# Keys in blocks of 128 and shared remainders in a three-stage attention kernel on one Trainium2 core

## The chip, the cores and the metric

The kernel runs on one core of a Trainium2 chip. The metric is the device time of one execution in microseconds (us); the median of the runs is compared. The engines are called by the names of the profile: PE multiplies matrices, DVE and POOL do elementwise work, ACT evaluates functions such as tanh and exp, SP issues most DMAs. DVE, ACT and POOL each work through their queue in order.

## What is computed

Three layers follow one another, all in float32. The first is soft-capped attention over 4 batches and 12 heads, 448 positions, 64 features per head. The second mixes four single-head causal attentions ("experts") of the 768 features, of which two are kept per position. The third is a gated feed-forward layer with a product along the positions.

```python
scores = scale * np.matmul(q, k.transpose(0, 1, 3, 2))      # (4, 12, 448, 448)
scores = cap * np.tanh(scores / cap)
attn = np.exp(scores - np.max(scores, axis=-1, keepdims=True))
attn = attn / (np.sum(attn, axis=-1, keepdims=True) + 1e-09)
x = np.matmul(attn, v)            # heads side by side: (4, 448, 768)
q, k, v = x @ wq[e], x @ wk[e], x @ wv[e]                   # per expert e
out += mask[..., None] * w * (softmax(causal(q @ k.T / 8)) @ v @ wo[e])
h = gelu(x @ w_in); u, v = halves of h                      # third layer
gated = u * (einsum('ts,bsd->btd', w_sg, layernorm(v)) + b_sg)
return x + gated @ w_out
```

## The kernel before

The unit of the first layer is a pair of heads: 24 pairs, six to a batch. The features of the two heads lie in the lower and the upper 64 partitions of one tile (`qp`, `kp`), so that two products of 64 rows each, one per head, can stand in the array at once. Scores are computed transposed, keys by queries. The 448 keys are cut into four blocks of 112 (`CP`, `NC`).

`slot(i, side)` (line 253) is one step of the program, and its calls write the order of the queues out by hand; until the end of the first layer PE, DVE, ACT and POOL keep the order in which the calls stand (`InOrder`, `pin`). Slot i holds: the first two key blocks of pair i (`scores(..., 0, ...)`, line 192), with a tanh per block and one exp for both; the values of pair i - 1 (`values`, line 219), in which four blocks of 112 keys are accumulated for both heads into one tile `po`; the last two blocks of pair i; after each second pair a product with a one-hot matrix (`sums`, line 230) that adds up the exp over the keys; and the additions of the four blocks of exp into `pb` (`add_up`, line 214). The first of them, block 0 plus block 1, stands in `scores` (line 208): it is done by DVE in batch 0 and by POOL after it. The other two are done by DVE.

Between these stand the calls `side("a")`, `side("w")`, `side("p")` and `side("n")`, which put the rest of the program into the slots. In slots 0 to 9 (`prepare_weights`, line 574) that is the product of `wo` and `w_in`: DVE turns twelve units of 64-bit words into float32 (`convert`, six kinds of operation, tiles `wi..m`, `wi..e`), and PE multiplies them (`products`, tiles `w2ps`), by the tables `turns`, `u_loads` and `u_products`. From slot 10 on it is the second layer of the batch before (`PLAN`, line 481): `queries_keys` (tiles `qk`), `values_chunk` (`v`), `weigh` (`a`, `pe`), `turn` (`tr`, `pt`), `attend` (`av`).

`normed` (line 318) takes a finished batch from the first layer to the second. `invert` takes the reciprocal of the sums, writes it to DRAM and reads it back spread over partitions (`rb`); `over_sums` multiplies the attention output `os` by it; `in_parts` splits the result into a rounded part `xh` and a rest `xl`, three pieces of two feature blocks each. The products `qk` read `xh` and `xl` and begin in slot 10 (for batch 0).

After the last slot (24) the order is no longer held by hand: `experts_end` (line 559) and the third layer (`mlp_a`, `mlp_b`, `mlp_c`) are interleaved, and a scheduler sets the order. PSUM, the memory that PE writes to, is divided into two two-bank tiles for scores (`ps_s`), one bank for `po` (`ps_o`) and three for all else (`ps_g`, tag "g").

The lines that fix the shape of the work:

```python
mm(s[:CP, j, :S], kp[r, c * CP:(c + 1) * CP], qp[r, :], start=True, stop=True)      # scores
mm(po[64 * j:64 * j + 64, :S], vv[:, j, c, :], pend[b, hp][c // 2][:, j, c % 2, :], # values
   start=(c == 0), stop=(c == NC - 1))
(dve if b == 0 else pool_e).tensor_tensor(pb, p[:, :, 0, :], p[:, :, 1, :], op=ALU.add)
```

Of the kernel before, what the change touches and what calls it, by code (L numbers as in the profile page):

```python
# [22 lines left out]
HP = H // 2  # L23
# [5 lines left out]
CP, NC = 112, 4  # L29
EPS = 1e-9  # L30
# [42 lines left out]
def build(ctx: ExitStack, tc: tile.TileContext, a: dict):  # L73
# [55 lines left out]
    onehot = const.tile([CP, 3, 32], F32, name="onehot")  # L129
# [47 lines left out]
    os_t, sums_t, pend, rb_d = {}, {}, {}, {}  # L177

    def load_pair(b, hp):

        qp = at.tile([128, S], F32, tag="qp", name=f"qp{b}_{hp}", bufs=3)
        kp = at.tile([128, S], F32, tag="kp", name=f"kp{b}_{hp}", bufs=3)
        vv = at.tile([CP, 2, NC, D], F32, tag="vv", name=f"vv{b}_{hp}", bufs=3)
        nc.sync.dma_start(kp, a["kT"][b, :, hp, :])
        nc.sync.dma_start(qp, a["qT"][b, :, hp, :])
        if (b, hp) == pairs[0]:
            scale()
            load_w(0)
        nc.sync.dma_start(vv, a["v"][b, :, 2 * hp:2 * hp + 2])
        return qp, kp, vv  # L190

    def scores(b, hp, h, qp, kp):

        p = at.tile([CP, 2, 2, S], F32, tag="p", name=f"p{b}_{hp}_{h}", bufs=4)
        for c2 in range(2):
            c = 2 * h + c2
            s = ps_s.tile([128, 2, 512], F32, tag="s", name=f"s{b}_{hp}_{c}")
# [16 lines left out]
    def add_up(b, hp):
        _, p, pb = pend[b, hp]
        for c2 in range(2):
            dve.tensor_tensor(pb, pb, p[:, :, c2, :], op=ALU.add)

    def values(b, hp, vv):
        po = ps_o.tile([128, 512], F32, tag="po", name=f"po{b}_{hp}")  # L220
# [690 lines left out]
```

## Time and profile before

| | us |
|---|---|
| median of 3 runs | 558.57 |
| lowest, highest | 557.87, 561.39 |
| the profiled execution | 559.72 |
| span of its trace | 558.0 |

The span runs from the first to the last instruction of the program; the profiled execution's own time lies 1.7 us above it. A row of a view names the engine, the operation and the tiles as out<-in. Line 119 of the kernel is the helper that issues every matmul, line 104 the one for all of DVE, ACT and POOL, so groups are told apart by their tiles. A float32 matmul shows as two instructions. Ends of matmuls are modelled and overlap, so the distance from start to start is what a group costs PE.

### The profile page before, as it was taken

To read this page: it belongs to the slowest core of one execution; us is meant where nothing else is said; L and a number is where in the kernel's file an instruction comes from. 1 tells how busy PE (TensorE), PEld (TensorE's weight loads), DVE (VectorE), ACT (ScalarE), POOL (GpSimd) and SP (SyncE) were. 2 spreads that over 40 slices of the span, in tenths; PEclk is the share of its full clock that TensorE was granted. 3 is DMA by queue.
4 is the path that set the end of the run, shared out by engine and by line. 5 is a ranking of instruction groups with operands and counts; after the bars stand their busy time and mean duration, and the time that the engine had idled before them with its cause. 6 is when DMAs were issued, how large, how long until landed. Compare 5 with 4: busy or idle time off the path is not lost.

```text
span 558.0 us, 7562 instructions
## 1 busy us (share of the span) xinstructions
PE 532.7 (95%) x2732; PEld 346.3 (62%) x2732; DVE 361.4 (65%) x725; ACT 325.7 (58%) x508; POOL 141.4 (25%) x180
## 2 busy tenths in 40 slices
PE   7999999899999989999988989999999989999997
PEld 2333333455555554656557655878768879889996
DVE  3899999984666636567567599676631786485300
ACT  5988888688687896577822345353534344253211
POOL 0000122141155251243340364515521131031000
PEclk9999999999999999999999978999999999999999
DMA  8974615752424141322056221010421000000111
GB/s 246 338 217 123 207 51 160 223 175 80 130 67 142 50 140 49 103 71 67 22 158 165 54 59 58 29 58 0 162 101 64 2 0 34 33 34 33 51 49 66
DMA packets 30596, 53.97 MB, mean 97 GB/s; under 512 B 3872, under 2 KB 22880, under 8 KB 30560
## 3 DMA queue, kind: packets, MB, share of 16 engines
q1 hardware_dynamic: 29408, 48.26, 28.2%
q0 software_dynamic: 1152, 5.24, 2.8%
q8 instruction: 21, 0.34, 0.3%
q14 instruction: 15, 0.12, 0.1%
HBM read 41.83 MB, written 11.67 MB: 96 GB/s over the span
## 4 chain that ended last, share of the span: by engine, by line
PE 73%; DVE 16%; ACT 6%; DMA 2%; issue 2%; POOL 1%; DVEq 0%; POOLq 0%; ACTq 0%; SPq 0%
PE o L119 15%; PE po L119 10%; PE s L119 10%; PE qk L119 8%; PE sp L119 7%; PE v L119 5%; ACT p L104 4%; PE a L119 3%; PE hv L119 3%; PE hu L119 3%; PE w2ps L119 2%; PE tr L461 2%; PE av L119 2%; DVE pb L104 2%; DVE rs L104 2%
## 5 line engine op out<-in xcount | busy, mean ns | idle before, releaser
L104 ACT ACTIVATE p<-s,tsc 112x896 f32<-112x896 f32 x96 | 91.4, 1005 | 24.4 <-PE s L119 24.4
L119 PE MATMUL s<-qp,kp 64*112 64x448 f32 x384 | 84.4, 557 | 3.4 <-ACT p L104 3.4
L104 ACT ACTIVATE p<-p,capt 112x1792 f32<-112x1792 f32 x48 | 85.9, 1790 | 1.3
L104 POOL TENSOR_TENSOR pb<-p 112x896 f32<-112x896 f32 x18 | 38.9, 2163 | 166.6 <-ACT p L104 96.9
L119 PE MATMUL po<-p,vv 112*64 112x448 f32 x384 | 77.3, 545 | 0.0
L104 DVE TENSOR_TENSOR pb<-pb,p 112x896 f32<-112x896 f32 x48 | 57.3, 1194 | 16.0 <-ACT p L104 12.3
L119 PEld LDWEIGHTS s<-qp,kp 64*112 64x112 f32 x384 | 30.8, 172 | 50.6 <-issue 21.3
L119 PEld LDWEIGHTS po<-p,vv 112*64 112x64 f32 x384 | 25.5, 136 | 45.0 <-issue 44.0
L104 ACT ACTIVATE pe<-a,m 112x112 f32<-112x112 f32 (+3 forms) x64 | 31.2, 491 | 25.3 <-DVE m L104 24.5
L104 POOL TENSOR_SCALAR pe<-pe,cs 112x112 f32<-112x112 f32 (+1 forms) x64 | 31.6, 519 | 50.3 <-DVE cs L104 50.2
L104 DVE CUSTOM_DVE_ANT_0 a<-a,neg 112x112 f32<-112x112 f32 (+3 forms) x64 | 27.7, 464 | 20.0 <-PE a L119 20.0
L119 PE MATMUL qk<-xh,wqk_h 128*128 128x448 f32 x96 | 38.2, 398 | 2.6 <-DVE xh L104 2.6
L119 PE MATMUL o<-gh,wu_h 128*128 128x448 f32 x96 | 35.6, 371 | 0.8 <-DMA wu_h<-wud 0.8
L119 PE MATMUL o<-gl,wu_h 128*128 128x448 f32 x96 | 35.6, 371 | 0.0
L119 PE MATMUL qk<-xh,wqk_l 128*128 128x448 f32 x96 | 35.4, 369 | 0.0
L119 PE MATMUL a<-qk 64*112 64x112 f32 (+3 forms) x128 | 29.9, 440 | 5.6 <-ACT pe L104 3.4
L119 PE MATMUL o<-gh,wu_l 128*128 128x448 f32 x96 | 35.0, 370 | 0.0
L104 ACT ACTIVATE ob<-o 128x448 f32<-128x448 f32 x24 | 13.0, 541 | 31.5 <-PE o L119 31.3
L119 PE MATMUL v<-wvg_h,xh 128*112 128x260 f32 x96 | 28.7, 299 | 0.7 <-ACT pe L104 0.7
L461 PE MATMUL tr<-ident,pe 112*112 112x112 f32 x160 | 23.7, 261 | 4.9 <-DVE lg L104 1.8
L119 PE MATMUL v<-wvg_h,xl 128*112 128x260 f32 x96 | 27.1, 283 | 0.0
L119 PE MATMUL v<-wvg_l,xh 128*112 128x260 f32 x96 | 27.1, 282 | 0.0
(226 smaller groups left out, 1096.5 us busy)
## 6 DMA issues: line engine op xcount, KB each, us to landing
kp<-in_kT_dram SPq DMA_DIRECT2D x24, 224.0 KB, 3.1
qp<-in_qT_dram SPq DMA_DIRECT2D x24, 224.0 KB, 3.2
vv<-in_v_dram SPq DMA_DIRECT2D x24, 224.0 KB, 3.1
rb<-rd SPq DMA_DIRECT2D x24, 224.0 KB, 4.7
out_dram<-ob SPq DMA_DIRECT2D x24, 224.0 KB, 1.9
wuw<-in_w_out_dram SPq DMA_DIRECT2D x8, 384.0 KB, 3.5
wud<-wuw SPq DMA_DIRECT2D x16, 192.0 KB, 1.9
ws<-in_wqk_dram SPq DMA_DIRECT2D x4, 384.0 KB, 6.0
```

What stands on the lines that cost most here:

```text
L104: ins = f(*args, **kw)
L119: pin(nc.tensor.matmul(*args, **kw))
L461: pin(nc.tensor.transpose(g[:CP, j * CP:(j + 1) * CP], pe[:, j * CP:(j + 1) * CP], ident))
```

## The change

The keys are cut into three blocks of 128 (`KT` is 384) and a remainder of 64. The remainders of an even pair and of the odd pair after it make one block, computed in the slot of the odd pair: even pair in the lower, odd pair in the upper 64 partitions of the scores. Its products have 64 rows and 64 columns, so four of them, two pairs by two heads, stand in quarters of the array. The values of a pair are computed two slots after its scores; those of an odd pair begin with the four quarter products, of which two finish `po` of the even pair and two open `po` of the odd pair. `po` of odd pairs lies in `ps_g`. A slot is added (slot 25) for the values of pair 23.

All additions into `pb` are done by DVE now: two for an even pair, four for an odd one, of which two have 64 partitions. In `normed`, batch 0 is taken over earlier, and in `prepare_weights` the products stand up to one slot earlier and `wt` is loaded ahead of the first units. The loads are put into other places of the slots; the values' remainder is a load of its own (`vl`).

```diff
+KT = S - S % 128
...
+    def load_v(i):
...
+        b, hp = pairs[i]
+        vv = at.tile([128, 2, KT // 128, D], F32, tag="vv", name=f"vv{i}", bufs=3)
         nc.sync.dma_start(vv, a["v"][b, :, 2 * hp:2 * hp + 2])
...
+        vl = None
+        if hp % 2:
+            vl = at.tile([128, 2, D], F32, tag="vl", name=f"vl{i}", bufs=2)
+            nc.sync.dma_start(vl, a["vl"][b, hp // 2])
...
+    def scores(i, h):
+        last = h == 1 and i % 2 == 1
+        n = 2 if h == 0 or last else 1
+        p = at.tile([128, 2, n, S], F32, tag=("p0", "p1" if n == 1 else "p2")[h], name=f"p{i}_{h}", bufs=(3, 1)[h])
+        pend[i] = (*pend.get(i, ()), p)
+        for c2 in range(n):
+            s = ps_s.tile([128, 2, 512], F32, tag="s", name=f"s{i}_{2 * h + c2}")
             for j in range(2):
                 r = slice(64 * j, 64 * j + 64)
+                if c2 and last:
+                    for half in range(2):
+                        qp, kp = qk_t[i - 1 + half]
+                        mm(s[64 * half:64 * half + 64, j, :S], kp[r, KT:], qp[r, :], start=True, stop=True)
+                else:
+                    qp, kp = qk_t[i]
+                    c = 2 * h + c2
+                    mm(s[:, j, :S], kp[r, c * 128:(c + 1) * 128], qp[r, :], start=True, stop=True)
+            act.activation(p[:, :, c2, :], s[:, :, :S], AF.Tanh, scale=tsc)
             yield 805.0
+        act.activation(p, p, AF.Exp, scale=capt)
...
+    def add_up(i, h):
+        p = pend[i][h]
         if h == 0:
+            pb = pbs[i] = at.tile([128, 2, S], F32, tag="pb", name=f"pb{i}", bufs=3)
+            dve.tensor_tensor(pb, p[:, :, 0, :], p[:, :, 1, :], op=ALU.add)
+            return
+        dve.tensor_tensor(pbs[i], pbs[i], p[:, :, 0, :], op=ALU.add)
+        if i % 2:
+            for half in range(2):
+                r, pb = slice(64 * half, 64 * half + 64), pbs[i - 1 + half]
+                dve.tensor_tensor(pb[r], pb[r], p[r, :, 1, :], op=ALU.add)
+    def values(i):
+        vv, vl = v_t.pop(i)
+        odd = i % 2
+        po = po_t[i] = (ps_g if odd else ps_o).tile([128, 512], F32, tag="g" if odd else "po", name=f"po{i}")
+        if odd:
+            b, hp = pairs[i]
+            p = pend[i][1]
+            for half in range(2):
+                r = slice(64 * half, 64 * half + 64)
+                for j in range(2):
+                    mm(po_t[i - 1 + half][64 * j:64 * j + 64, :S], vl[r, j, :], p[r, j, 1, :],
+                       start=(half == 1), stop=(half == 0))
+            os_t[b, hp // 2] = ao.tile([128, 2, S], F32, tag="os", name=f"os{i}", bufs=4)
+            act.activation(os_t[b, hp // 2][:, 0, :], po_t.pop(i - 1)[:, :S], AF.Copy)
+        for c in range(KT // 128):
             for j in range(2):
+                mm(po[64 * j:64 * j + 64, :S], vv[:, j, c, :], pend[i][c // 2][:, j, c % 2, :],
+                   start=(c == 0 and not odd), stop=(c == KT // 128 - 1 and odd == 1))
             yield 805.0
+        if odd:
+            act.activation(os_t[b, hp // 2][:, 1, :], po_t.pop(i)[:, :S], AF.Copy)
...
+        if i > 1:
+            drain(values(i - 2))
+        if here:
+            load_v(i)
         side("a")
...
+        if here:
+            add_up(i, 0)
+            drain(scores(i, 1))
...
-        elif step == (3, "w"):
+        elif step == ((3, "w") if b else (2, "a1")):
             over_sums(b, 0)
             over_sums(b, 1)
             load_rb(b, 2)
-        elif b == 0 and step == (3, "a1"):
+        elif b == 0 and step == (3, "w"):
             in_parts(b, 0)
             in_parts(b, 1)
-        elif step == (4, "w"):
-            if b:
-                in_parts(b, 0)
+        elif b == 0 and step == (3, "n"):
             over_sums(b, 2)
-            if not b:
-                in_parts(b, 2)
+            in_parts(b, 2)
+        elif b and step == (4, "w"):
+            in_parts(b, 0)
+            over_sums(b, 2)
         elif b and step == (4, "a1"):
             in_parts(b, 1)
...
-        u_products = [(), (), (0,), (1, 2), (3,), (4, 5), (6,), (7, 8), (9,), (10, 11)]
+        u_products = [(), (0,), (1,), (2,), (3, 4), (5,), (6, 7), (8,), (9,), (10, 11)]
```

How the instructions stand on an engine is shown at three places. The first is PE in slot 5 (pair 5 of batch 0). `s` are scores with the pair and the block in the name, `po` values; before, the name has the batch and the pair in it.

```order
L119 MATMUL s0_5_0_429<-qp5_297,kp5_298 112x448 x2
L119 MATMUL s0_5_1_433<-qp5_297,kp5_298 112x448 x2
L119 MATMUL po0_4_453<-p0_4_0_369,vv0_4_337 64x448 x4
L119 MATMUL po0_4_453<-p0_4_1_404,vv0_4_337 64x448 x4
L119 MATMUL s0_5_2_476<-qp5_297,kp5_298 112x448 x2
L119 MATMUL s0_5_3_480<-qp5_297,kp5_298 112x448 x2
```

The same slot in the changed kernel:

```order
L120 MATMUL s5_0_406<-qp5_342,kp5_343 128x448 x2
L120 MATMUL s5_1_410<-qp5_342,kp5_343 128x448 x2
L120 MATMUL po2_377<-p3_1_330,vl3_317 64x448 x2
L120 MATMUL po3_428<-p3_1_330,vl3_317 64x448 x2
L120 MATMUL po3_428<-p3_0_278,vv3_315 64x448 x4
L120 MATMUL po3_428<-p3_1_330,vv3_315 64x448 x2
L120 MATMUL s5_2_458<-qp5_342,kp5_343 128x448 x2
L120 MATMUL s5_3_462<-qp4_224,kp4_225 64x448
L120 MATMUL s5_3_462<-qp5_342,kp5_343 64x448
L120 MATMUL s5_3_462<-qp4_224,kp4_225 64x448
L120 MATMUL s5_3_462<-qp5_342,kp5_343 64x448
```

The odd slot has 10 score products and 10 value products, against 8 and 8 before; an even one has 6 and 6, so two pairs keep 16 and 16. Quarter products are the two rows that read `vl3` and the four of `s5_3`.

The second place is DVE in slots 7 and 8, from the first addition for pair 7 (before: pair 1 of batch 1) to the first product with `rb` of batch 0. Before:

```order
L104 TENSOR_TENSOR pb1_1_587<-pb1_1_587,p1_1_1_622 112x896 x2
L104 TENSOR_SCALAR wi11m_652<-wi1_5w_528 128x512
L104 TENSOR_SCALAR wi11m_652<-wi11m_652 128x512 x2
L104 SCALAR_TENSOR_TENSOR wi11m_652<-wi1_5w_528,wi11m_652 128x512
L104 TENSOR_SCALAR wi11e_653<-wi11m_652 128x512
L104 SCALAR_TENSOR_TENSOR wi11e_653<-wi1_5w_528,wi11e_653 128x512
L104 TENSOR_TENSOR wi11m_652<-wi11m_652,wi11e_653 128x512
L104 TENSOR_TENSOR wqk_l_76<-ws7_589,wqk_h_75 128x6x128
L104 COPY rs1_696<-sum1_0_691 128x448
L104 TENSOR_TENSOR pb1_2_662<-pb1_2_662,p1_2_1_679 112x896 x2
L104 TENSOR_TENSOR wqk_l_76<-ws8_664,wqk_h_75 128x6x128
L104 TENSOR_TENSOR os0_0_217<-os0_0_217,rb0_0_616 128x896
```

In the changed kernel:

```order
L105 TENSOR_TENSOR pb7_602<-p7_0_545 128x896
L105 TENSOR_TENSOR pb7_602<-pb7_602,p7_1_604 128x896
L105 TENSOR_TENSOR pb6_524<-pb6_524,p7_1_604 64x896
L105 TENSOR_TENSOR pb7_602<-pb7_602,p7_1_604 64x896
L105 TENSOR_SCALAR wi11m_639<-wi1_5w_513 128x512
L105 TENSOR_SCALAR wi11m_639<-wi11m_639 128x512 x2
L105 SCALAR_TENSOR_TENSOR wi11m_639<-wi1_5w_513,wi11m_639 128x512
L105 TENSOR_SCALAR wi11e_640<-wi11m_639 128x512
L105 SCALAR_TENSOR_TENSOR wi11e_640<-wi1_5w_513,wi11e_640 128x512
L105 TENSOR_TENSOR wi11m_639<-wi11m_639,wi11e_640 128x512
L105 TENSOR_TENSOR wqk_l_76<-ws7_564,wqk_h_75 128x6x128
L105 TENSOR_TENSOR os1_306<-os1_306,rb0_0_596 128x896
```

An odd pair has four additions where it had two, and the row that reads only `p7_0` was POOL's. The first product with `rb` moves ahead of pair 8's additions and of the second `wqk_l` row.

The third place is PE at the end of the first layer, from the last `sums` on. `a` are expert scores of batch 2, `hv` and `hu` the first products of the third layer. Before:

```order
L119 MATMUL sum3_2_2432<-pb3_5_2251,onehot_71 32x448 x2
L119 MATMUL a2_0_0_2_2491<-qk2_0_2197 112x336
L119 MATMUL a2_0_1_2_2492<-qk2_0_2197 112x336
L119 MATMUL a2_0_0_3_2516<-qk2_0_2197 112x448
L119 MATMUL a2_0_1_3_2517<-qk2_0_2197 112x448
L119 MATMUL hv0_0_2509<-w2_h_2462,yh0_2503 112x512
```

In the changed kernel:

```order
L120 MATMUL sum3_2_2418<-pb23_2271,onehot_71 32x448 x2
L120 MATMUL a2_0_0_2_2424<-qk2_0_2177 112x336
L120 MATMUL a2_0_1_2_2425<-qk2_0_2177 112x336
L120 MATMUL po22_2336<-p23_1_2273,vl23_2257 64x448 x2
L120 MATMUL po23_2436<-p23_1_2273,vl23_2257 64x448 x2
L120 MATMUL po23_2436<-p23_0_2208,vv23_2255 64x448 x4
L120 MATMUL po23_2436<-p23_1_2273,vv23_2255 64x448 x2
L120 MATMUL a2_0_0_3_2450<-qk2_0_2177 112x448
L120 MATMUL a2_0_1_3_2451<-qk2_0_2177 112x448
L120 MATMUL v2_2_2471<-wvg_h_77,xh2_2139 112x260
```

The values of pair 23 stand between the two steps of `weigh`; they were done one slot earlier.

## Rows read from the trace of the kernel before

**Rows 1.** The page, part 1: busy time, share of the span, instructions.

```profile
PE 532.7 (95%) x2732; PEld 346.3 (62%) x2732; DVE 361.4 (65%) x725; ACT 325.7 (58%) x508; POOL 141.4 (25%) x180
```

**Rows 2.** Busy time per stretch; columns: PE, PEld, DVE, ACT, POOL, clock, DMA, GB/s.

```profile
24.20:110.30 86.10, 83.51 (x359) 30.84 (x358) 83.03 (x113) 73.16 (x68) 10.97 (x5) 1.00 0.56 170
111.50:290.40 178.90, 174.65 (x1031) 99.35 (x1030) 108.76 (x246) 131.84 (x192) 60.65 (x62) 1.00 0.31 95
322.00:558.00 236.00, 225.09 (x1111) 187.69 (x1109) 134.76 (x293) 93.61 (x210) 60.00 (x93) 0.96 0.14 49
```

**Rows 3.** The chain that ended last, 60 to 125 us: start, length, what.

```profile
69.61 1.01 DVE pb L104
...
108.59 0.64 DVE xh L104
...
109.27 2.31 PE qk L119 x10
```

**Rows 4.** The timeline of PE, 60 to 73 us: start, length, instructions.

```profile
63.41 1.76 PE L119 MATMUL s<-qp,kp 64*112 64x448 f32 x8
65.10 1.98 PE L119 MATMUL w2ps<-wi6m,wt 128*128 128x512 f32 x4
67.02 0.96 PE L119 MATMUL sum<-pb,onehot 112*32 112x448 f32 x8
67.91 1.76 PE L119 MATMUL s<-qp,kp 64*112 64x448 f32 x8
69.60 3.23 PE L119 MATMUL po<-p,vv 112*64 112x448 f32 x16
72.75 0.63 PE L119 MATMUL s<-qp,kp 64*112 64x448 f32 x2
```

**Rows 5.** Groups of DVE, then of POOL, 24.2 to 110.3 us: busy us, mean ns.

```profile
L104 DVE TENSOR_TENSOR pb<-pb,p 112x896 f32<-112x896 f32 x17 | 22.8, 1342 | 0.3
L104 DVE TENSOR_TENSOR pb<-p 112x896 f32<-112x896 f32 x4 | 4.3, 1084 | 0.0
...
L104 DVE SCALAR_TENSOR_TENSOR wi9m<-wi_3w,wi9m 128x512 int32<-128x512 int32 x1 | 2.5, 2451 | 0.0
L104 DVE TENSOR_SCALAR wi8m<-wi8m 128x512 f32<-128x512 f32 x1 | 2.2, 2189 | 0.0
...
L104 DVE SCALAR_TENSOR_TENSOR wi5m<-wi_5w,wi5m 128x512 int32<-128x512 int32 x1 | 0.7, 693 | 0.0
...
L104 DVE TENSOR_SCALAR wi4m<-wi4m 128x512 f32<-128x512 f32 x1 | 0.4, 428 | 0.0
...
L104 POOL TENSOR_TENSOR pb<-p 112x896 f32<-112x896 f32 x5 | 11.0, 2194 | 92.8 <-DVE pb L104 61.8 <-ACT p L104 23.2 <-PE po L119 7.9
```

**Rows 6.** The timeline of PE, 103 to 119 us.

```profile
109.27 0.48 PE L119 MATMUL qk<-xh,wqk_h 128*128 128x448 f32 x1 [2.59 <-DVE xh L104]
...
111.51 0.96 PE L119 MATMUL sum<-pb,onehot 112*32 112x448 f32 x8
```

**Rows 7.** Busy time per stretch, 320 to 350 us; columns as in rows 2.

```profile
320.00:330.00 10.00, 7.30 (x36) 5.04 (x37) 8.28 (x16) 4.95 (x15) 6.22 (x7) 0.81 0.30 82
340.00:350.00 10.00, 8.73 (x23) 5.42 (x22) 9.33 (x29) 6.83 (x16) 2.82 (x5) 0.66 0.14 41
```

**Rows 8.** Groups of DVE, 111.5 to 290.4 us, of the form of the additions.

```profile
L104 DVE TENSOR_TENSOR pb<-pb,p 112x896 f32<-112x896 f32 x28 | 31.2, 1115 | 13.9 <-ACT p L104 10.6 <-POOL pb L104 2.8
```

**Rows 9.** The timeline of PE, 288.5 to 301 us.

```profile
289.48 0.96 PE L119 MATMUL sum<-pb,onehot 112*32 112x448 f32 x8
290.37 1.81 PE L119 MATMUL a<-qk 64*112 64x336 f32 x6
292.92 1.00 PE L119 MATMUL a<-qk 64*112 64x448 f32 x2 [0.73 <-ACT pe L104]
293.85 1.18 PE L119 MATMUL hv<-w_h,yh 128*112 128x512 f32 x4
```

**Rows 10.** The timeline of PE at 187 us, expert scores that wait for nothing.

```profile
187.33 0.73 PE L119 MATMUL a<-qk 64*112 64x336 f32 x4
```

More of the change, by code (lines that the diff above doesn't have):

```diff
@@ L192, in scores, with load_qk @@
[L192 to L197, printed above, removed]
+    os_t, sums_t, pend, pbs, rb_d = {}, {}, {}, {}, {}
+    pairs = [(b, hp) for b in range(B) for hp in range(HP)]
+    qk_t, v_t, po_t = {}, {}, {}
+    def load_qk(i):
+        b, hp = pairs[i]
+        qk_t[i] = [at.tile([128, S], F32, tag=t, name=f"{t}{i}", bufs=3) for t in ("qp", "kp")]
+        nc.sync.dma_start(qk_t[i][1], a["kT"][b, :, hp, :])
+        nc.sync.dma_start(qk_t[i][0], a["qT"][b, :, hp, :])
@@ L214, in add_up @@
[L214 to L220, printed above, removed]
-        for c in range(NC):
+            pb = pbs[i] = at.tile([128, 2, S], F32, tag="pb", name=f"pb{i}", bufs=3)
+            dve.tensor_tensor(pb, p[:, :, 0, :], p[:, :, 1, :], op=ALU.add)
+            return
+        dve.tensor_tensor(pbs[i], pbs[i], p[:, :, 0, :], op=ALU.add)
@@ L248, in invert @@
             load_rb(b, h2)
-    pairs = [(b, hp) for b in range(B) for hp in range(HP)]
-    ld = {}
     def slot(i, side):
+        here = i < len(pairs)
         if i == 0:
-            ld[0] = load_pair(*pairs[0])
-            ld[1] = load_pair(*pairs[1])
-        if i + 2 < len(pairs):
-            qk = [at.tile([128, S], F32, tag=t, name=f"{t}{i + 2}", bufs=3) for t in ("qp", "kp")]
-            b, hp = pairs[i + 2]
-            nc.sync.dma_start(qk[1], a["kT"][b, :, hp, :])
-            nc.sync.dma_start(qk[0], a["qT"][b, :, hp, :])
-            ld[i + 2] = qk
-        if i < len(pairs):
-            first = scores(*pairs[i], 0, *ld[i][:2])
+            load_qk(0)
+            scale()
+            load_w(0)
+            load_qk(1)
+        if i % 2 == 0 and i + 2 < len(pairs):
+            load_qk(i + 2)
+        if here:
+            first = scores(i, 0)
             drain(islice(first, 2))
@@ L289, in slot @@
                 drain(sums(b, hp // 2))
-        if i < len(pairs):
-            add_up(*pairs[i])
+        if here:
+            add_up(i, 1)
         side("n")
@@ L652, in build @@
     YA = {}
-    for n in range(PRE_SLOTS, B * HP + 1):
+    for n in range(PRE_SLOTS, B * HP + 2):
         slot(n, beside(n))
@@ L882, in _layout @@
     r = np.arange(CP)
[L883 removed]
+    hot = np.zeros((128, 3, 32), np.float32)
     for i in range(3):
```

55 lines of the change are left out of this document (13 added, 42 removed).

## The prediction

> **What bounds the kernel now.** I read the page first, then the busy time per stretch, then the chain, and last the timelines of the two places where the chain changes engines. The page shows PE busy for 95% of the span [rows 1]. Its matmuls overlap, so that share alone does not make PE the bound; the stretches tell more [rows 2]. From 24.2 to 110.3 us, the slots that also prepare weights, PE is busy for 83.5 of 86.1 us and DVE for 83.0, the rest of DVE's time being gaps between its 113 operations. Two engines are full at once. The chain leaves PE for DVE at 69.6 us and returns to PE only when the last `xh` is written, at 109.27 [rows 3]; PE waits 2.59 us for it in the middle of the first `qk` group [rows 6]. So in this stretch DVE sets the end. From 111.5 to 290.4 us, the rest of the first layer beside the second, PE is busy for 174.7 of 178.9 us, DVE for 108.8 and ACT for 131.8 [rows 2]; here PE is the bound. What follows, 236 us of it from 322 us on, the change leaves alone but for what the scheduler makes of it.
>
> **The price of a group on PE.** Start to start, 8 score instructions take 1.69 us (63.41 to 65.10), 16 value instructions 3.15 (69.60 to 72.75), and the 8 of `sum` only 0.89 (67.02 to 67.91) [rows 4]. Scores and values keep two products in the array at once, by rows or by columns, so these groups are 4 and 8 steps of two instructions; `sum` uses strips of 32 columns and makes 2 steps of four. With 0.37 us a step and 0.18 for entering a group the three come to 1.66, 3.14 and 0.92. The array therefore did hold four products when they lay in four column strips, and two by rows; no row has both splits together. I take a quarter group (8 instructions) at 2 steps and an entry, 0.92 us. The other bound is two at a time, 4 steps, 1.66.
>
> The entry is a cost that the change adds to. The Trainium skill, TensorEngine Tiling (Array Packing), Key Properties, says that changing the tiling mode drains the engine, which speaks against a group in quarters between groups in halves; it gives no price, and the trace's 0.18 us agrees in kind. The same section says that tiles work independently and in parallel, which no row here shows for quarters; by it the group would be the 0.92 us above.
>
> **The change on PE.** The instructions stay 16 score and 16 value products per two pairs; only the steps shrink. Scores of two pairs: 16 steps and 4 entries before, 14 and 5 after. Values: 16 and 2 before, 14 and 3 after. That is 4 steps less and 2 entries more, 1.48 - 0.36 = 1.12 us per two pairs and 13.4 us for all twelve. Where each part falls decides how much arrives.
>
> **Preparation stretch, -3.6.** PE gets ahead, but the additions that were POOL's move to DVE, which is full. Eight pairs (2 to 9) had 16 + 4 additions on DVE and have 24: 4 more at 1.084 us, +4.3 [rows 5]. Against that, DVE no longer meets POOL's additions, of 2.19 us each. Five DVE operations have lengths that only such a meeting explains: 17 additions average 1.342 instead of about 1.08, 4.4 us together; one `wi9m` takes 2.451 where its like takes 0.693, and one `wi8m` 2.189 against 0.428 [rows 5]: 4.4 + 1.76 + 1.76 = 7.9 us. DVE's end comes 7.9 - 4.3 = 3.6 us earlier, and with it the end of the first `qk` group (111.51 [rows 6]). The reordered take-over of batch 0 puts nothing else behind the last `xl`. The products being one slot earlier, and the loads in another order, I take at nothing: the conversions that feed them are DVE's, whose queue is what is late. If a load is late in the first 20 us it costs up to 2; a start without waits gains up to 1. So -1 to -5.
>
> PE's own saving there, some 6 us by pair 10, is hidden; it becomes a longer wait for `xh`. In addition one pair's values have moved behind this point. Such a wait can cost clock. The granted clock was 0.81 from 320 to 330 us, when PE had been busy for only 7.3 of 10 us, and 0.66 from 340 to 350 [rows 7], a mix of 1.2 and 2.4 GHz. Ten us at 0.66 lose 3.4, nothing lowered loses 0; I take +1.0, as the wait is one and not several.
>
> **Second stretch, -7.1.** Before, its scores are pairs 11 to 23 and its values pairs 10 to 23; after, the values are 9 to 22. Scores: pair 11 is an odd slot and pays one entry more, six double pairs save 2 steps and pay one entry: 12 steps less, 7 entries more, 4.44 - 1.26 = 3.2. Values: 14 groups of 8 steps (112 steps, 14 entries) become 8 + 84 + 6 = 98 steps and 2 + 18 + 1 = 21 entries: 5.18 - 1.26 = 3.9. Sum 7.1, all on PE, which is the bound here.
>
> DVE gets 13 further additions of 1.08 us in it, some 14 us, and stays at 123 of 172 us. They stand in its queue ahead of small operations that the second layer waits for (copies of `tr`, the gates). If none of that shows it is 0 or better, since 2.8 us of DVE's wait for POOL's `pb` go [rows 8]; if all shows it is +14. The idle time, over a quarter, speaks for the low end: +0.5. ACT's work shrinks by an eighth (7 blocks instead of 8), and it is not the bound in either stretch; nothing. `po` of odd pairs takes one of three banks that `a`, `v` and `tr` rotate through; its copy by ACT follows at once and 10 us of other work lie between, so nothing.
>
> **After the first layer, +1.5.** The values of pair 23 (8 steps, 2 entries, 3.3 us) now stand between the two steps of `weigh`. Between these PE had stalled: six `a` instructions began at 290.37 and the last two only at 292.92, `hv` at 293.85 [rows 9], 3.48 in all. Four that wait for nothing take 0.73 at 336 columns [rows 10] and in proportion 0.97 at 448, so 1.7 is work and 1.8 waiting. The values fill the wait: 3.3 - 1.8 = +1.5, at least 0, at most 3.3.
>
> **Sum.** -3.6 + 1.0 - 7.1 + 0.5 + 1.5 = -7.7 us. The profiled execution took 559.7 us (span 558.0 and 1.7 around it) and would take 552.0; it lies 1.1 above the median of the runs, so the median becomes 558.6 - 7.7 = 550.9. A measurement of this kernel tells about 1%, 5.6 us, from no change.
>
> **Rivals.**
> - Quarters run two at a time. For it: no row has both splits. Against it: `sum`'s four at once. Each quarter group costs 2 steps, 0.74, more. In the preparation stretch DVE still covers that; in the second, 7 + 7 groups cost 10.4, and pair 23's one 0.7: 550.9 + 11.1 = 562.0.
> - DVE's longer queue becomes the bound in the second stretch. Place: odd slots, where the reciprocal, four additions and the gates stand ahead of the next `settle`. It decides once the additions delay PE by their whole length: +14 instead of +0.5, 564.4, to which `wum` conversions in the same queue can add 1 or 2: slower than before, about 566. Against it: 70 us of DVE idle there [rows 2].
> - PE's saving arrives whole, because DVE's queue in the preparation stretch shortens by more than counted: -13.4 with +1.5 and +0.5, about 547, or 545.5 if the wait in pair 23's slot covers all.
> - The saving is lost in part later: the order after the last slot is the scheduler's, the low clock sits there [rows 7], and a shift of a few us either way gives 553 to 558.
>
> **How the numbers follow.** Forecast 0.45 (its own range 548 to 553); whole saving 0.15; lost in part 0.20; quarters in twos 0.11; DVE the bound 0.09. Faster by over 1% is below 553.0: 0.45 + 0.15 = 0.60. Slower by over 1% is above 564.2: 0.08 of the DVE case. The rest, 0.32, lies within 1%. The range 543 to 562.5 leaves out the DVE case and the far side of the whole saving and of the quarters.
>
> **What would show it.** Right: a quarter group of 8 instructions takes about 0.9 us start to start; no DVE operation over 2 us but the reciprocal between 24 and 105 us; the first `qk` group ends near 108 us after a wait for `xh` of 4 us or more; the last `sum` of batch 3 starts near 280 us instead of 289.5. Wrong: a quarter group of 1.6 us or more; PE waiting for DVE by over 8 us in the second stretch; a last `sum` at 284 or later; or a time from there to the end that grows by more than 4 us.

## The result: 1.15% slower, and the profile after

The changed kernel takes 565.41 us (median of 6 runs, 563.73 to 566.38) against 558.76 for the kernel before, a ratio of 1.0115 with an interval of 1.0098 to 1.0132. The forecast was 550.9, range 543.0 to 562.5: wrong in sign and outside the range. The profiled execution took 565.89 us, span 564.0 (before 558.0).

Cut at two events that both kernels have, the start of the first `sum` behind the first `qk` group and the start of the last `sum` of batch 3, the spans compare so:

| us | before | after | difference | forecast |
|---|---|---|---|---|
| to the first `sum` behind `qk` | 111.51 | 113.36 | +1.9 | -2.6 |
| second stretch, to the last `sum` | 177.97 | 179.91 | +1.9 | -6.6 |
| from there to the end | 268.5 | 270.7 | +2.2 | +1.5 |

Busy time in part 1 of the page, beside [rows 1]: PE fell by 8.1 us, DVE rose by 14.9, ACT and POOL fell.

```profile
PE 524.6 (93%) x2732; PEld 337.1 (60%) x2732; DVE 376.3 (67%) x743; ACT 304.0 (54%) x496; POOL 112.0 (20%) x162
```

The first stretch of [rows 2], columns as there (PE, PEld, DVE, ACT, POOL, clock, DMA, GB/s), then the second stretch from `sum` to `sum`, in the kernel before and in the changed one:

```profile
24.20:110.30 86.10, 80.36 (x346) 26.32 (x343) 77.73 (x114) 62.49 (x61) 0.00 (x0) 0.96 0.51 161
```

```profile
111.51:289.48 177.97, 173.72 (x1022) 99.16 (x1021) 108.07 (x244) 131.74 (x192) 60.65 (x62) 1.00 0.31 94
```

```profile
113.36:293.27 179.91, 168.43 (x1026) 94.70 (x1025) 121.37 (x258) 120.94 (x186) 37.37 (x47) 1.00 0.30 91
```

Between the two `sum`s PE is busy for 5.3 us less than before, where the forecast took off 7.1, and idle for 7.2 us more (11.5 against 4.2): the stretch gets 1.9 longer. Added up start to start without the waits, scores and values do fall by 7.3 us together; PE's other groups, with the same instructions and the same clock of 1.00, take 1.9 longer. Why they do was not followed up.

**What the groups cost.** The timeline of PE at the place that answers to [rows 4], an odd slot; 8 scores, 8 quarter products of the values, 12 values, then 12 scores of which the last 8 are quarters:

```profile
114.25 1.77 PE L120 MATMUL s<-qp,kp 64*128 64x448 f32 x8
115.95 0.98 PE L120 MATMUL po<-p,vl 64*64 64x448 f32 x8
116.86 2.48 PE L120 MATMUL po<-p,vv 128*64 128x448 f32 x12
119.27 1.94 PE L120 MATMUL s<-qp,kp 64*128 64x448 f32 x12
121.14 0.47 PE L120 MATMUL qk<-xh,wqk_h 128*128 128x448 f32 x1
```

A quarter group takes 0.91 us start to start (115.95 to 116.86; forecast 0.92, and 1.66 if two ran at a time): four products do run at once. The odd slot's values take 3.32 and its scores 1.70 + 1.87; with the even slot's 2.41 and 1.70 + 0.95 two pairs cost 11.95 us, where [rows 4] give 4 x 1.69 + 2 x 3.15 = 13.06. The saving is 1.11 us per two pairs; forecast 1.12.

**Where the first stretch lost it.** PE in slot 9 (pair 9), from 85 us:

```profile
85.03 1.77 PE L120 MATMUL s<-qp,kp 64*128 64x448 f32 x8
86.74 0.97 PE L120 MATMUL po<-p,vl 64*64 64x448 f32 x4
92.59 1.76 PE L120 MATMUL po<-p,vl 64*64 64x448 f32 x4 [4.89 <-DVE rs L105]
94.28 4.75 PE L120 MATMUL po<-p,vv 128*64 128x448 f32 x12
98.95 1.94 PE L120 MATMUL s<-qp,kp 64*128 64x448 f32 x12
```

The quarter group is torn in two. Its first half closes `po` of pair 6, in its own bank; its second half opens `po` of pair 7, which needs a bank of the tag "g", and waits 4.89 us for DVE's `rs`. From 86.74 to 98.95 the values take 12.2 us instead of 3.3. What DVE does at the end of that wait:

```profile
88.05 0.95 DVE L105 TENSOR_TENSOR wqk_l<-ws,wqk_h 128x768 fp32r<-128x768 f32 x1
88.92 2.08 DVE L105 TENSOR_TENSOR os<-os,rb 128x896 f32<-128x896 f32 x2
90.92 1.08 DVE L105 TENSOR_TENSOR pb<-p 128x896 f32<-128x896 f32 x1
91.92 0.62 DVE L105 COPY rs<-sum 128x448 f32<-128x448 f32 x1
```

DVE does not idle; it comes to the copy of the sums, which frees the bank, seven us after PE went on from `sum` to the next scores (85.03). Of three banks the two `w2ps` tiles hold two for six units on end, so `sum` and the new `po` share the third. The granted clock around the wait (columns as above):

```profile
85.00:90.00 5.00, 2.71 (x14) 0.88 (x12) 4.83 (x9) 3.87 (x4) 0.00 (x0) 1.00 0.64 172
90.00:95.00 5.00, 2.41 (x6) 0.58 (x8) 4.97 (x7) 0.26 (x1) 0.00 (x0) 0.71 0.53 171
95.00:100.00 5.00, 5.00 (x20) 1.34 (x20) 3.70 (x4) 0.54 (x1) 0.00 (x0) 0.60 0.32 93
```

PE waits, then works on at the lower level: the last 12 value products take 4.67 us (94.28 to 98.95) instead of 2.41. Then DVE in its turn idles 5.8 us, for `w2h`, which ACT can't make before PE has made `w2ps`:

```profile
L105 DVE TENSOR_TENSOR pb<-p 128x896 f32<-128x896 f32 x8 | 8.6, 1077 | 0.0
...
L105 DVE TENSOR_TENSOR w2l<-w2ps,w2h 128x512 fp32r<-128x512 f32 x4 | 2.7, 688 | 5.8 <-ACT w2h L105 5.8
```

DVE had been freed of POOL, as forecast: its 24 additions take 1.08 us each, and no operation but the reciprocal exceeds 1.5 us, where [rows 5] has additions of 1.34 on average and two operations of 2.2 and 2.5.

**Where the second stretch lost it.** What PE waits for between the two `sum`s, by engine and tile (us in total, times, longest), in the kernel before (111.5 to 289.5) and in the changed one (113.3 to 293.3):

```profile
PE tr L461 <- DVE lg L104: 1.8, 2, 1.5
PE tr L461 <- DVE pt L104: 1.1, 1, 1.1
PE a L119 <- ACT qk L104: 0.9, 1, 0.9
PE s L119 <- ACT p L104: 0.4, 1, 0.4
```

```profile
PE s L120 <- ACT p L105: 2.6, 2, 2.2
PE tr L487 <- DVE pt L105: 2.4, 3, 2.1
PE tr L487 <- DVE lg L105: 1.5, 2, 1.2
PE tr L487 <- ACT y L105: 1.5, 1, 1.5
PE tr L487 <- POOL pe L105: 1.5, 1, 1.5
PE qk L120 <- DVE xh L105: 0.9, 2, 0.5
PE a L120 <- ACT qk L105: 0.7, 1, 0.7
PE a L120 <- ACT pe L105: 0.4, 1, 0.4
```

That is 4.2 us before and 11.5 after. The rows of ACT `p`, ACT `y` and POOL `pe`, 5.6 us together (0.4 before), lie at the change from slot 13 to 14 and from 19 to 20. First ACT, then DVE at 13:

```profile
148.78 0.38 ACT L105 ACTIVATE vp<-v 112x256 f32<-112x256 f32 x1 [0.21 <-PE v L120]
153.92 0.22 ACT L105 ACTIVATE wt<-wt 112x16 f32<-112x16 f32 x1 [4.75 <-DVE wt L105]
154.04 1.89 ACT L105 ACTIVATE p<-s,tsc 128x896 f32<-128x896 f32 x2
```

```profile
149.20 0.16 DVE L105 COPY lg<-v 112x4 f32<-112x4 f32 x1 [0.43 <-ACT vp L105]
149.28 3.18 DVE L105 TENSOR_TENSOR pb<-pb,p 128x896 f32<-128x896 f32 x3
152.47 0.23 DVE L105 TENSOR_TENSOR gt<-lg 112x64 f32<-112x64 f32 x1
```

DVE copies `lg`, then does three additions (two before the change), then the gates. ACT needs `wt` from the gates and stands 4.75 us with two tanh behind it in its queue, and PE, itself 0.7 us quicker through its values, waits 2.23 us for the first tanh. `settle`, which makes `cs` and with it `pe`, follows the gates in DVE's queue, and PE waits 1.45 us for `pe`.

### The profile page after: what moved, and what is told of

Its sections match the earlier page's. It is cut to its first block, busy times and chain, and to the rows that moved or that the text cites. A ratio compares the mean times of both kernels' runs of the same rounds, so it can differ in the third digit from the quotient of the medians.

```text
span 564.0 us, 7562 instructions
## 1 busy us (share of the span) xinstructions
PE 524.6 (93%) x2732; PEld 337.1 (60%) x2732; DVE 376.3 (67%) x743; ACT 304.0 (54%) x496; POOL 112.0 (20%) x162
## 4 chain that ended last, share of the span: by engine, by line
PE 54%; DVE 26%; ACT 6%; DMA 6%; POOL 3%; issue 3%; SPq 0%; DVEq 0%; POOLq 0%; ACTq 0%
PE o L120 14%; DVE pb L105 7%; PE po L120 6%; PE sp L120 5%; PE s L120 5%; PE v L120 5%; PE qk L120 4%; ACT p L105 4%; PE a L120 3%; DMA rb<-rd 3%; PE hv L120 2%; PE hu L120 2%; PE tr L487 2%; DVE rs L105 2%; DVE vg L105 2%
## 5 line engine op out<-in xcount | busy, mean ns | idle before, releaser
L105 ACT ACTIVATE p<-s,tsc 128x896 f32<-128x896 f32 x84 | 81.0, 1004 | 30.9 <-PE s L120 29.9
L120 PE MATMUL s<-qp,kp 64*128 64x448 f32 (+1 forms) x384 | 79.3, 578 | 5.6 <-ACT p L105 5.6
L105 ACT ACTIVATE p<-p,capt 128x1792 f32<-128x1792 f32 (+1 forms) x48 | 77.0, 1604 | 1.3
L120 PE MATMUL po<-p,vv 128*64 128x448 f32 x288 | 61.5, 564 | 0.0
L105 DVE TENSOR_TENSOR pb<-pb,p 128x896 f32<-128x896 f32 (+1 forms) x48 | 51.0, 1084 | 13.5 <-ACT p L105 12.9
L120 PEld LDWEIGHTS s<-qp,kp 64*128 64x128 f32 (+1 forms) x384 | 27.4, 175 | 51.8 <-issue 20.6
L105 POOL TENSOR_SCALAR wuw<-wum 128x384 fp32r<-128x384 f32 x8 | 7.0, 872 | 181.2 <-DVE wum L105 173.6
L120 PEld LDWEIGHTS po<-p,vv 128*64 128x64 f32 x288 | 19.1, 140 | 36.8 <-issue 35.8
L105 DVE TENSOR_TENSOR pb<-p 128x896 f32<-128x896 f32 x24 | 27.9, 1162 | 3.8 <-ACT p L105 3.8
L120 PEld LDWEIGHTS a<-qk 64*112 64x112 f32 x128 | 12.3, 173 | 25.6 <-issue 10.2
```

Source lines behind the costliest of these rows:

```text
L105: ins = f(*args, **kw)
L120: pin(nc.tensor.matmul(*args, **kw))
```

## Experiments

All runs in one table: median, ratio to the kernel before beside which each was run, and the three parts of the profiled span as above. The parts are those of one execution each, which can lie up to 3 us from the median (565.01 in run 3, 558.68 in run 16). "Changed" is the changed kernel, "before" the kernel before; "+" adds an edit.

| kernel | us | ratio (interval) | first | second | rest |
|---|---|---|---|---|---|
| before | 558.8 | 1 | 111.5 | 178.0 | 268.5 |
| changed | 565.41 | 1.0115 (1.0098 to 1.0132) | 113.4 | 179.9 | 270.7 |
| 1 changed + copy on ACT | 560.28 | 1.0018 (0.9989 to 1.0047) | 106.7 | 181.6 | 270.5 |
| 2 changed + gates first | 570.45 | 1.0194 (1.0143 to 1.0244) | 112.7 | 183.1 | 271.4 |
| 3 changed + POOL from pair 6 | 567.86 | 1.0146 (1.0086 to 1.0205) | 115.1 | 176.5 | 271.6 |
| 4 = 1 + gates first | 562.84 | 1.0059 (1.0033 to 1.0086) | 106.6 | 181.2 | 273.7 |
| 5 = 1 + four additions behind settle | 560.21 | 1.0014 (0.9991 to 1.0037) | 106.7 | 180.7 | 269.1 |
| 6 = 1 + three additions behind settle | 560.40 | 1.0026 (1.0006 to 1.0046) | 106.6 | 180.2 | 272.4 |
| 7 before + additions on DVE | 573.37 | 1.0268 (1.0242 to 1.0295) | 108.6 | 197.9 | 265.3 |
| 8 changed, `normed` as before | 563.42 | 1.0092 (1.0057 to 1.0126) | 110.1 | 179.9 | 270.2 |
| 9 = 1 + POOL from pair 10 | 562.89 | 1.0078 (1.0051 to 1.0104) | 109.4 | 178.9 | 274.0 |
| 10 = 1 + three additions behind `pt` | 554.29 | 0.9927 (0.9902 to 0.9952) | 106.6 | 176.8 | 267.9 |
| 11 = 10 + POOL from pair 10 | 556.32 | 0.9953 (0.9930 to 0.9976) | 109.2 | 174.8 | 271.1 |
| 12 before + additions on DVE, at the end | 564.67 | 1.0114 (1.0087 to 1.0142) | 109.3 | 187.3 | 266.1 |
| 13 = 10 + `xh` early | 552.04 | 0.9888 (0.9834 to 0.9941) | 104.4 | 177.2 | 268.1 |
| 14 = 10 + POOL from pair 12 | 553.82 | 0.9911 (0.9884 to 0.9939) | 106.7 | 176.4 | 269.7 |
| 15 = 13 + POOL from pair 12 | 551.08 | 0.9868 (0.9823 to 0.9914) | 103.7 | 175.1 | 271.0 |
| 16 = 10 + pair 23's values in slot 24 | 556.18 | 0.9963 (0.9935 to 0.9990) | 106.7 | 181.1 | 268.7 |
| 17 before + copy on ACT, `xh` early | 556.64 | 0.9978 (0.9951 to 1.0005) | 109.8 | 178.9 | 267.4 |

**1: the copy of the sums on ACT.** One line, in `sums`:

```diff
-            dve.tensor_copy(sums_t[b], g[:, :S])
+            act.activation(sums_t[b], g[:, :S], AF.Copy)
```

> The changed kernel with one edit: the copy of the first sums of a batch (rs<-sum) is done by ACT instead of DVE. Theory, a shared bank: in the preparation slots the two w2ps tiles hold two of the three banks of tag g, so po of an odd pair has to wait until the sum before it is copied out, and that copy stands in DVE's queue behind weights and the products with rb. Then the 4.9 us wait in the middle of po (92.6 us) goes, the granted clock from 24 to 110 us is 1.00 instead of 0.96, the first sum after the first qk group starts near 107 instead of 113.4, and the time falls by 5 to 8.9 us, to 556.5 to 560.4. Rival, a late load or late exp is what po waits for: a wait of 4 us or more stays at the same place under another name and the time is within 2 us of 565.4.

560.28, at the lower end of the forecast gain. PE at the same place:

```profile
85.95 0.98 PE L120 MATMUL po<-p,vl 64*64 64x448 f32 x8
86.86 2.48 PE L120 MATMUL po<-p,vv 128*64 128x448 f32 x12
...
103.75 0.47 PE L120 MATMUL qk<-xh,wqk_h 128*128 128x448 f32 x1 [2.04 <-DVE xh L105]
```

The values are whole again; moving one copy takes 6.7 us from the first stretch. The shared bank is shown, and the late load or exp of the rival is out. The first `sum` starts at 106.7, 4.8 us earlier than before the change, and PE waits for `xh` as the forecast had it, but 2.04 us instead of over 4, with a lower clock behind it (0.66 from 105 to 110 us). The second stretch grew by 1.7 us, though its waits fell from 11.5 to 9.6: PE's busy time rose by 3.5 us (168.4 to 171.9) for the same work. The granted clock, 1.00 throughout in the changed kernel, was 0.66 also from 220 to 225 us and 0.71 from 150 to 155.

**8: the order of `normed` as it was.** The three places of `over_sums` and `in_parts` for batch 0 go back to those of the kernel before.

> The changed kernel with the order of normed for batch 0 as it was before. The two products with rb (2.1 us) then stand behind the copy of the sums in DVE's queue instead of ahead of it. Shared-bank theory: PE's wait in po falls from 4.9 to about 2.9 us, since DVE is late by the rest too, and the time by 2 to 4 us: 561.5 to 563.5. Rival, the earlier products with rb are what makes xh ready in time: the wait falls but the first qk group ends no earlier than 113 us and the time is 565 or more.

563.42; the wait is 2.9 us, as expected. So 2 of the 4.9 us came from moving the products with `rb` (2.08 us) ahead of the copy. The other 2.9 stay with the old order: DVE is late there all the same.

**2 and 4: the gates ahead of the additions.** In slots 13, 19 and 25 `side("n")`, which issues the gates, stands ahead of `add_up(i, 1)`.

> The changed kernel with one edit: in slots 13, 19 and 25 the gates of the second layer stand ahead of the additions into pb, not behind them. Theory, place in the queue: what the second stretch lost is the three additions between the copies of lg and the gates; ACT's exp of wt, the tanh behind it, and POOL's pe all wait for them. Then PE's waits for ACT p (2.6), POOL pe (1.5) and ACT y (1.5) between 113 and 293 us nearly go, and the time falls by 4 to 6 us, to 559.4 to 561.4. Rival, the amount: DVE has 14 us more work there and PE is held up by it wherever it stands; then the waits come back under other names and the time stays within 1.5 us of 565.4.

> The changed kernel with both edits: the first copy of the sums on ACT, and the gates ahead of the additions in slots 13, 19 and 25. Theory: the two losses lie in different stretches and add, 565.4 - (5 to 8.9) - (4 to 6), 551 to 556, faster than the kernel before. Rival, one of them is hidden by the other or the time after the first layer takes it back: 557 or more.

570.45 and 562.84: slower by 5.0 and 2.6 us than without this edit. This theory fell, and so did its rival. The wait for ACT `p` went, and this came (run 2):

```profile
155.80 0.31 PE L491 MATMUL tr<-ident,pe 112*112 112x112 f32 x1 [2.01 <-DVE cs L105]
157.13 0.62 PE L491 MATMUL tr<-ident,pe 112*112 112x112 f32 x2 [1.02 <-POOL pe L105]
```

`turn` needs `pe`, POOL makes it with `cs`, and `cs` comes from DVE's `settle`, which stands behind the same additions as before. The same additions reached PE one step later: 3.0 us here instead of 3.7, and 9.9 instead of 11.5 in the stretch. That the stretch still grew by 3.2 us is clock: PE is busy for 173.0 us instead of 168.4, at a granted 0.61 and 0.70 from 155 to 165 us and 0.78 and 0.88 from 225 to 235, where the changed kernel has 1.00. In run 4 the second stretch stays as in run 1; its rest is 3.2 longer, and why isn't shown.

**5 and 6: behind `settle`.** `add_up` of slots 13 and 19 (all four additions in 5, the last three in 6) is called in the next slot, behind `settle`.

> The changed kernel with the first copy of the sums on ACT, and in slots 13 and 19 all four additions into pb put off until the second layer's settle in the next slot has been issued. The gates alone ahead of the additions only moved PE's wait from ACT p to DVE cs and POOL pe, which come from settle, one step further on. Theory, place in the queue: with gates and settle both ahead, PE's waits for ACT p, DVE cs, POOL pe and ACT y between 107 and 288 us fall together from 5.6 us to under 2; the time is 3 to 6 us under the 560.3 of the kernel with only the copy moved, 554.5 to 557.5. Rival, the amount of DVE's work: the additions come due behind settle, ahead of the copies pt, and PE waits for those instead; 559 or more.

> The same with only the three last additions put off, the first staying behind the reciprocal. Theory: the first addition stands in idle time of DVE in slot 13 but ahead of pt in slot 19, so this is within 1 us of the other, 555 to 558.5. Rival as there: 559 or more.

560.21 and 560.40: no gain over run 1. Two POOL rows show why for run 5; first the kernel before, then run 5, the eight multiplications of `pe`, which in run 5 five additions of DVE stand beside, and what PE does then:

```profile
233.46 3.84 POOL L104 TENSOR_SCALAR pe<-pe,cs 112x112 f32<-112x112 f32 x8 [12.42 <-DVE cs L104]
```

```profile
147.07 8.13 POOL L105 TENSOR_SCALAR pe<-pe,cs 112x112 f32<-112x112 f32 x8 [29.90 <-DVE cs L105]
```

```profile
153.74 0.78 PE L492 MATMUL tr<-ident,pe 112*112 112x112 f32 x3 [3.70 <-POOL pe L105]
```

In run 6 the eight take 7.30 us, and PE waits 0.9 for `pe` and 4.0 for `pt` (2.0 in run 1), as the rival had it. DVE and POOL prolong each other either way; the forecast had counted only POOL's harm to DVE. The Trainium skill, SBUF — State Buffer, Who interferes with whom, says that an instruction of DVE with two inputs in SBUF contends with one of POOL that reads SBUF, that this contention is an exclusive lock, and that the order of issue decides who is blocked; the 8.13 us against 3.84 agree.

**10: behind `pt`.** The additions wait until the copies `pt` of the next slot are issued, and `sums` of that pair of pairs moves one slot on, so that it doesn't wait for them:

```diff
+        late = lambda n: n in (13, 19)
+        if late(i - 2):
+            b, hp = pairs[i - 2]
+            drain(sums(b, hp // 2))
...
-            if hp % 2 == 1:
+            if hp % 2 == 1 and not late(i - 1):
                 drain(sums(b, hp // 2))
-        if here:
+        if late(i - 1):
+            add_up(i - 1, 1)
+        if here and not late(i):
             add_up(i, 1)
```

> The changed kernel with the first copy of the sums on ACT, and in slots 13 and 19 the last three additions put off until after the copies pt of the next slot, with the sums of that pair of pairs one slot later. Put off to a place just behind settle, the additions had met POOL's eight pe instructions, which took 8.1 us instead of 3.8, and PE waited for these. Theory: now nothing that PE waits for stands behind the additions or beside them; the waits for ACT p, POOL pe and ACT y go, the stretch from the first sum (106.7) to the last takes 175 to 177 instead of 181.6, the time is 554 to 557. Rival, the amount of DVE's work: 559 or more.

554.29, faster than both kernels. POOL's eight take this, as in run 1 (4.65):

```profile
146.76 4.66 POOL L105 TENSOR_SCALAR pe<-pe,cs 112x112 f32<-112x112 f32 x8 [29.68 <-DVE cs L105]
```

The second stretch falls by 4.8 us against run 1 with the same work on every engine; run 1, then run 10:

```profile
106.70:288.29 181.59, 171.94 (x1026) 97.38 (x1025) 118.55 (x256) 122.10 (x188) 37.34 (x47) 0.98 0.30 90
```

```profile
106.60:283.41 176.81, 168.74 (x1026) 94.92 (x1025) 119.98 (x255) 122.22 (x188) 37.38 (x47) 1.00 0.30 92
```

PE's waits for ACT `p`, ACT `y` and POOL `pe` fall from 4.1 to 0.8 us, those for `pt` rise from 2.0 to 3.8, and all together fall only from 9.6 to 8.1. The other 3.2 us are PE's busy time: behind the waits of run 1 the clock was lower, here it is 1.00 from 110 us on. These are one execution each, and that of run 10 is the fastest of its four; the medians are 6.0 us apart.

**3, 9, 11, 14: the first addition back to POOL,** from pair 6, 10, 10 and 12 on.

> The changed kernel with the first addition of each pair from pair 6 on given back to POOL. Theory, place in the queue: the addition given back is not among the three that stand ahead of the gates, so the waits for ACT p, POOL pe and ACT y stay; only PE's wait for pt (2.1 us) shrinks by 1 for an addition less behind the reciprocal. In the preparation slots DVE meets POOL again and the five long operations return. Together 563 to 568. Rival, the amount of DVE's work: 18 additions fewer on DVE bring back most of what the second stretch lost, and the time is 560 or less.

> The changed kernel with the first copy of the sums on ACT and the first addition of pairs 10 to 23 given back to POOL, that is only after the preparation slots. Giving it back from pair 6 on had shortened the second stretch from 179.9 to 176.5 us and lengthened the preparation slots by 1.7. Theory, the two stretches want different engines for this addition: the first sum after the preparation starts near 106.7 us, the second stretch takes 176 to 178, the time is 555 to 558. Rival, half clock after other waits takes it back: 559 or more.

> Both of these together with the copy on ACT. Theory: the waits that each removes are different ones (pt behind the reciprocal and one addition; gates behind three), 552 to 555, faster than the kernel before. Rival, POOL's additions of 2.1 us come to lie beside its pe work or prolong DVE's gates: 557 or more.

> The kernel with the copy on ACT and the late additions, and the first addition of pairs 12 to 23 given back to POOL. If the amount of DVE's work still costs something in the second stretch when the critical places are clear, this is faster: the wait for pt in slot 19 (2.0 us) halves, 551.5 to 553.5. If only places matter, the rest is within noise, 553.5 to 555.

Run 3 shortened the second stretch by 3.4 us and lengthened the first by 1.7; its median is 2.4 above the changed kernel's, which its one profile (of its quickest execution, span 0.8 below the changed kernel's) doesn't show. In runs 9 and 11 pair 10's addition still falls beside the last additions of the preparation: one of 64 partitions took 2.9 us in run 9, and the first `sum` came 2.7 and 2.6 later than in runs 1 and 10. For run 11 that is more than the 1.3 us by which it missed; run 9 missed by 4.9, and its rest, 3.5 longer than in run 1, isn't explained. With the places clear and the start at pair 12, run 14 differs from run 10 by half a microsecond, within both intervals. The wait for `pt` falls from 3.8 to 1.1 us, but that for `xh` rises from 0.9 to 2.1: on the whole the amount of DVE's work costs nothing there that these runs could tell.

**7 and 12: this part of the change alone, in the kernel before.**

```diff
-            (dve if b == 0 else pool_e).tensor_tensor(pb, p[:, :, 0, :], p[:, :, 1, :], op=ALU.add)
+            dve.tensor_tensor(pb, p[:, :, 0, :], p[:, :, 1, :], op=ALU.add)
```

> The kernel before with one edit: the first additions into pb are done by DVE in all batches, none by POOL. By the prediction's terms the preparation slots give 7.9 - 4.3 = 3.6 us and the second stretch costs little: 555 to 556. By what the second stretch of the changed kernel shows, an addition more on DVE in each slot costs PE's waits for pt and tr 1 to 3 us there: 556 to 559. Rival, POOL's additions were free and DVE's are not: slower than 560.

> The kernel before with the first addition of the pairs from batch 1 on done by DVE, but at the end of the slot, ahead of the other two, not right behind the first exp. Done right behind the exp it cost 14.6 us. Theory, place in the queue: at the end of the slot DVE does not stand waiting for an exp with small operations of the second layer queued behind it; 558 to 565. Rival, the amount of DVE's work: 570 or more.

573.37, on the rival's side and far beyond its 560. The first stretch gains 2.9 us (forecast of the prediction 3.6), the second loses 19.9. The longest of PE's waits there:

```profile
PE a L119 <- ACT qk L104: 5.6, 2, 4.3
PE s L119 <- ACT p L104: 3.5, 2, 2.3
PE tr L461 <- DVE lg L104: 3.2, 2, 2.9
```

All waits there are 16.8 us against 4.2. The other 7.3 us of the 19.9 PE spends on the same work (busy 181.1 against 173.7), at a granted clock of 0.62 to 0.70 in four stretches of five us.

With the same additions at the end of the slot the loss is 5.9 us instead of 14.6. So 8.7 us hang on the place alone. The 5.9 that remain, with an addition more ahead of the gates as in the changed kernel, were not taken apart.

**13 and 15: the last `xh` earlier, and the best version.** In `normed` the last piece of batch 0 is taken over at (3, "p") instead of (3, "n"), ahead of the additions of slot 9:

> The kernel with the copy of the sums on ACT and the late additions (554.3), and in slot 9 the product with rb, xh and xl of the last piece of batch 0 ahead of the three additions of that slot. Theory: at the end of the preparation DVE's queue is what PE waits for; these three additions (3.2 us) stand ahead of the last xh, so PE's wait of 2.1 us and the half clock behind it (105 to 110 us at 0.69) go, the first sum starts at 103.5 to 104.5 instead of 106.6, the time is 550.5 to 552.5. Rival, the sum then waits for these additions instead, or the second stretch takes it back: 553.5 or more.

> Both of these together. If both effects are as forecast they add: 548.5 to 551. If POOL's additions meet the gates or the time after the first layer takes it back: 552 or more.

Run 13 starts the first `sum` at 104.4 us without a wait for `xh` and with a clock of 1.00 behind it; 552.04 is as forecast. Run 15 has the lowest median, 551.08, just above its forecast; its ratio, 0.9868 (0.9823 to 0.9914), isn't told from run 13's. Its two stretches, for comparison with [rows 2]:

```profile
24.20:103.70 79.50, 76.45 (x350) 27.13 (x348) 76.70 (x112) 62.77 (x63) 0.00 (x0) 1.00 0.56 181
103.70:278.80 175.10, 169.07 (x1029) 95.07 (x1032) 111.57 (x246) 122.33 (x188) 57.07 (x59) 1.00 0.31 94
```

**17: the control.**

> A control: the kernel before with two of the edits that helped the changed kernel, the copy of the sums on ACT and the last piece of batch 0 (product with rb, xh, xl) ahead of the additions of slot 9. In the kernel before DVE too was late by these additions (PE's 2.6 us wait for xh), but PE has no shorter groups to profit from it. If the 551 of the best version came from these edits alone: 552 or less. If the cut of the keys brings what its groups save on PE: the control takes 555 to 557.5, as only the wait of 2.6 us goes.

556.64, with an interval that holds 1: these edits bring the kernel before about one us, not told from none. The control lacks two more edits of run 15 that this kernel could take too. One is the late additions; of its waits in the second stretch, 4.2 us in all, only the 0.4 for ACT `p` is of the kind that they end. The other is DVE in POOL's place for pairs 6 to 11. The control's first stretch:

```profile
24.20:109.80 85.60, 85.13 (x366) 31.68 (x362) 81.13 (x110) 74.28 (x71) 14.86 (x5) 1.00 0.59 178
```

PE waits 0.5 us in it; in run 7, which has that edit, the first `sum` came at 108.6, 1.2 earlier, and in run 15 at 103.7. So most of the 5.6 us between this run and run 15 needs PE's shorter groups, that is the cut of the keys; the control with all the edits was not run.

**16: pair 23's values.**

> The kernel with the copy on ACT and the late additions, and the values of pair 23 in slot 24 right behind those of pair 22, not between the two steps of weigh in slot 25. The prediction held that they fill 1.8 us of a wait there, so that moving them out costs 1.8 us: 555.5 to 556.5. Rival, the wait in slot 25 is not one that other PE work fills (the order behind it shifts with it): 553.5 to 554.8.

556.18, 1.9 above run 10 with intervals that overlap a little. The traces say the same: from the first `a` behind the last `sum` to the next `v` run 16 takes 3.93 us (288.65 to 292.58), run 10 takes 5.05 (284.30 to 289.35) with 3.36 of values in it. So the values fill 2.2 us of waiting, 1.8 by the forecast.

## Why the prediction was wrong, step by step

- **The price of a quarter group** (0.92): right, 0.91. The rival of two at a time is out. The saving of 1.12 us per two pairs: right, 1.11.
- **DVE freed from POOL in the preparation, -3.6**: the mechanism was right. Run 7, where nothing else changes in that stretch, shows -2.9; with the bank cleared run 1, which also has the shorter groups and a copy less on DVE, shows -4.8.
- **"`po` of odd pairs takes one of three banks that `a`, `v` and `tr` rotate through ... so nothing"**: the first step that failed. It was reasoned for the second stretch and applied to both. In the preparation two of the three banks are held by `w2ps`, and the third is freed by DVE, the engine that the same prediction had called full. Measured: 6.7 us, the difference that run 1 makes to the first stretch, of which 4.9 are the wait.
- **The clock, +1.0**: a lowering was expected behind a wait for `xh`. The changed kernel has no such wait in the first `qk` group; the lowering came behind the wait for the bank, and cost 2.3 us on 12 value products alone.
- **PE in the second stretch, -7.1**: right for scores and values (-7.3), but PE's busy time fell by 5.3 only, because its other groups took 1.9 longer. The sum had no term for them, and the cause is open.
- **DVE's additions in the second stretch, "+0.5"**: the second step that failed, and the larger. The bounds were 0 and +14, and the low one was taken because DVE idles for a quarter of the stretch. Measured: PE's waits rose by 7.2 us, 6.7 more than the term; with the 1.8 of the line above that makes the 8.5 us by which the stretch missed its forecast. Of the 7.2, 5.2 are the waits for ACT `p`, ACT `y` and POOL `pe`, which run 10 all but removes, and 1.3 those for `pt`. The idle time was real but lay elsewhere: it says nothing on what stands between `lg` and the gates. The rival of the DVE bound had the place right (odd slots, additions ahead of `settle`) and got 0.09; its price, 14 us, was too high for the changed kernel. That run 7 lost 14.6 is no support for it: there the additions stand at another place, in another kernel, and 7.3 us of what its second stretch loses are clock.
- **"The end of the values of pair 23, +1.5"**: right. From the first `a` to what follows the last, the kernel before takes 3.48 us [rows 9] and the changed one 5.05 (294.16 to 299.21), +1.57, and run 16 agrees. The rest as a whole grew by 2.2. The other 0.6 is a balance of longer and shorter pieces, among them a wait of 5.4 us for one `pe` near 337 us (2.2 before); its cause wasn't tested. The last column of the table, 265 to 274 us over kernels most of which differ only ahead of this part, shows how far it moves without an edit to it.
- **The range**: it weighed the bank at nothing and had no rival for it. With that loss removed (run 1, 560.28) the time lies inside the range, but by luck: the term of the second stretch was still wrong.

That run 15 lands on the forecast of 550.9 doesn't make it right: it has a copy, twelve additions and two groups of operations in other places.

## What to carry to other kernels

When an instruction is moved to a busy in-order engine, price it by what stands behind it in the queue at each place, not by the engine's idle share of the stretch: in the kernel before, the same eighteen additions cost 14.6 us behind the first exp and 5.9 at the end of the slot, and in the changed one, with the places clear, twelve of them on DVE or on POOL made no difference that could be told. Read the granted clock beside the waits: a part of a loss or a gain can be the same work at another clock (3.2 of the 4.8 us between runs 1 and 10). When a tile is moved to another pool, count for each stage of the program who holds that pool's banks and which engine gives them back; a bank freed by the fullest engine is as late as that engine's queue. A saving on the bounding engine arrives only up to the next wait, so name that wait before adding the saving to a sum.

## What the runs showed of the chip that was not expected

- POOL's multiplications suffer from DVE's additions too: eight `pe` took 8.13 us beside five additions (run 5), 3.84 before, 4.66 with one beside them (run 10).
- An addition over 64 partitions takes DVE as long as one over 128: 1083 against 1085 ns in the preparation stretch.
- A wait of 2.0 us on PE (run 1, at 103.7) was followed by a granted clock of 0.66 over the next five us, one of 2.6 before the change, in the same `qk` group [rows 6], by none (1.00 from 110 to 115 us). Nor does the amount of waiting tell: the changed kernel waits 11.5 us in the second stretch at 1.00, run 1 waits 9.6 and has 0.66 to 0.94 in four stretches of five us. What decides it, these rows don't show.
